# Sign bits of sixteen 64-bit weight tiles masked on POOL, and two instead of three DVE operations in their conversion

## The chip, the core and the metric

The kernel runs on one core of a Trainium2 chip. TensorE (PE) multiplies, VectorE (DVE), ScalarE (ACT) and GpSimd (POOL) work elementwise, SyncE (SP) issues most transfers. Each engine works off its own row of instructions in order and waits for others by semaphores. The metric is the device time of one execution in microseconds (us); lower is better.

## The reference

Three stages follow each other on 6016 rows of 256: the real part of a two-dimensional Fourier transform, then two feed-forward layers of width 2048.

```python
X = np.fft.fft(np.fft.fft(x, axis=1), axis=2).real          # x: 2 x 3008 x 256
h = X @ w_in                                                # layer one, 256 -> 2048
g = np.maximum(h, 0.0) + alpha * np.minimum(h, 0.0)
x = g @ w_out                                               # 2048 -> 256
h = x @ w_in2                                               # layer two
g = h * (1.0 / (1.0 + np.exp(-h)))
out = g @ w_out2
```

The weights w_in, w_out, w_in2 and w_out2 come as 64-bit floats. The kernel gets them as pairs of 32-bit words and makes 32-bit floats of them itself.

## The kernel before

**Stages.** First a part of the Fourier transform is computed (the psU, psB and psP matmuls), then a loop of 96 steps does layer one: 6 blocks of columns (c) by 16 slices of the width (m). Layer two follows from about 500 us on. Steps 0 to 15 are the first block, and in them the weights of layer one arrive, are converted and, for w_in, mixed with the last Fourier matrix.

**One step of layer one** (`step1`): PE makes two products, psh, of three matmuls each. DVE computes h (L588), a sum and a difference in place in PSUM (L589, L591), ACT the negative parts r (L590, L592), and DVE adds them to the products (L594, twice: the first r and the second r). Then `close1`: ACT rounds r to gh (L610), POOL computes the rest, gl = r - gh (L611, the lo part), and second products pso (L626) of gh and gl are put in a queue; PE takes some of them between the psh products of the next steps. Three banks of PSUM serve psh, one bank (tag x) serves psW, psS, psB and others in turn.

**A conversion** (`narrow`): raw words arrive by DMA. ACT scales the high words into y (L227) and the low words in place (L228). Then DVE shifts y left by three (L233), adds the scaled low words (L235, shown as ISA or CUSTOM) and puts the sign bit of the high word in (L237). For w_in, y is the tile wq, and `mix_w` follows: matmuls psW (L536), ACT's hi part (L538), DVE's lo part (L551), and column sums psS (L542). For w_out, `halves` follows: ACT's hi part (L281) and POOL's lo part (L282). Three conversions lie before step 0. The other thirteen of layer one go with steps 0 to 11 and 13, w_in in steps 0, 2, 4, 6, 8 and 10 (even steps), w_out in 1, 3, 5, 7, 9, 11 and 13 (odd steps). The weights of layer two are converted later, from about 220 us on.

**What sets the order.** Everything is issued from one program in which the conversions are generators. They are advanced at fixed places of a step: EARLY at its start, AMID between the two psh products, MID1 between the two L594, MID2 and MID3 behind the second, LATE at the end. The counter `now[0]` is the step; `NF` is 16.

Of the kernel before, what the change touches and what calls it, by code (L numbers as in the profile page):

```python
# [14 lines left out]
ALU = mybir.AluOpType  # L15
# [10 lines left out]
NF = DFF // P  # L26
KG = 2
CK = 8
NC = B * H1 // CK
# [68 lines left out]
def kernel(  # L98
# [16 lines left out]
    V, A, G, T = nc.vector, nc.scalar, nc.gpsimd, nc.tensor  # L115
# [40 lines left out]
    def wtile(shape, dtype, name, tag):  # L156
        return work.tile(shape, dtype, name=name, tag=tag, bufs=BUFS[tag])
# [10 lines left out]
    EARLY, AMID, LATE, BANK, MID1, MID2, MID3 = range(1, 8)  # L168
# [11 lines left out]
    now, taken = [0], set()  # L180
# [17 lines left out]
    def load64(src, raw, eng=nc.sync):  # L198
        eng.dma_start(raw.rearrange("p a n t -> p a (n t)"), src.bitcast(I32))

    def place_raw():
        while started and held[3] == BUFS["raw"]:
            yield EARLY
        held[3] += 1

    def narrow(src, finish, raw=None, lead=0, y=None, ready=lambda: True):

        held[0] += 1
        mine = raw is None
        if mine:  # L210
            yield from place_raw()
            raw = wtile([P, *src.shape[1:], 2], I32, "raw64", "raw")
            load64(src, raw)
            for _ in range(LOAD if lead > 1 else 1 if not started else 2 if now[0] < NF else 1 + lead):
                yield EARLY
        low, high = raw[:, :, :, 0], raw[:, :, :, 1]
        while not ready():
            yield EARLY
        own = y is None
        while own and lead and held[1] == BUFS["y"]:  # L220
            yield EARLY
        held[1] += own
        y = wtile(list(low.shape), F32, "y64", "y") if own else y()
        yi = y.bitcast(I32)
        if started:
            yield AMID
        A.activation(y, high.bitcast(F32), AF.Copy, scale=2.0 ** -112)  # L227
        A.activation(low, low.bitcast(U32), AF.Copy, scale=2.0 ** -29)  # L228
        if now[0] >= NC * NF or not started:
            yield LATE  # L230
        far = NF <= now[0] < NC * NF
        yield MID2 if far else MID1
        V.tensor_scalar(yi, yi, 3, None, op0=ALU.logical_shift_left)  # L233
        yield MID2
        V.tensor_tensor(yi, yi, low, op=ALU.add)  # L235
        yield MID2 if far else MID3
        V.scalar_tensor_tensor(yi, high, -2147483648, yi, op0=ALU.bitwise_and, op1=ALU.bitwise_or)  # L237
        held[0] -= 1
        held[3] -= mine
        if lead >= 0 and started and now[0] < NC * NF:  # L240
            for _ in range(2 if now[0] else 1):
                yield EARLY
            yield AMID
        else:
            for _ in range(1 + lead):
                yield EARLY
        yield from finish(y)
        held[1] -= own
# [4 lines left out]
    def keep_back(src, key):  # L253
        def finish(y):
            stash[key] = dram.tile(list(y.shape), F32, name="stash_{}{}".format(*key))
            nc.sync.dma_start(stash[key], y)
            return
            yield

        return narrow(src, finish)  # L260
# [28 lines left out]
    def narrow_wout(src, dst, tag, n, lead=0, raw=None):  # L289

        q, m = divmod(2 * n, 4)

        def place():
            if m == 0:
                dst[q] = keep.tile([P, 4, 2, D], F32R, name=f"{tag}o{q}", tag=f"{tag}{q}")
            return dst[q][:, m:m + 2, 0, :], dst[q][:, m:m + 2, 1, :]

        if ("o", n) in stash and tag == "wA":
            return bring_back(("o", n), halves(place, (tag, n)), lead)
        return narrow(rows_wout(src, n), halves(place, (tag, n)), raw, lead)  # L300
# [14 lines left out]
    def narrow_win2(p, lead=0):  # L315
        def finish(y):

            a = y.rearrange("p k (m f) -> p k m f", m=2)
            four = y.rearrange("p k (m f) -> p (k m) f", m=2)
            while held[2]:  # L320
                yield EARLY
            held[2] = 1
            w = wi2[p] = place_win2(p)
            s = t1.rearrange("p (i f) -> p i f", i=4)
            A.activation(w[:, :4, 0], four, AF.Copy)
            SE.tensor_tensor(s[:, 0], a[:, 0, 1], a[:, 1, 1], op=ALU.add)
            SE.tensor_tensor(s[:, 1], s[:, 0], a[:, 0, 0], op=ALU.subtract)
            SE.tensor_tensor(s[:, 2], a[:, 0, 0], a[:, 0, 1], op=ALU.subtract)
            SE.tensor_tensor(s[:, 3], a[:, 1, 0], s[:, 1], op=ALU.subtract)
            G.tensor_tensor(w[:, :4, 1], four, f32(w[:, :4, 0]), op=ALU.subtract)  # L330
            for _ in range(1 + lead):
                yield EARLY
            A.activation(w[:, 4:, 0], s, AF.Copy)
            G.tensor_tensor(w[:, 4:, 1], s, f32(w[:, 4:, 0]), op=ALU.subtract)
            held[2] = 0

        if ("i", p) in stash:
            return bring_back(("i", p), finish, lead)
        return narrow(rows_win2(p), finish, None, lead)
# [789 lines left out]
```

## Time and profile before

| | |
|---|---|
| three runs | 977.17, 977.41, 981.92 us (median 977.41) |
| profiled execution | 981.92 us, of it 980.1 us span from the first to the last instruction |
| PE, DVE, ACT, POOL busy | 97%, 73%, 61%, 52% of the span |
| mean granted TensorE clock | 0.993 of full speed |
| L233, L235, L237 in the first 130 us | 16 each, 0.42, 0.69 and 0.69 us by the median |
| POOL L611 (gl) in steps 0 to 15 | 16 of 2.17 us |

In an order of time each row has the start in us from the span's beginning, the duration in us, the engine, line and operation, the tiles written and read, and their shape; in brackets stands how long the engine had been idle before and what released it. Durations include the time in which an operation was held up after its start; with operations that overlap in the pipeline the next one starts before the bar of the last ends.

### The profile page before, as it was taken

Reading aid. Unit: us, or ns where it says so; the run is one execution under the profiler, and the core shown is the slowest. Engines: PE = TensorE matmul, PEld = TensorE weight load, DVE = VectorE, ACT = ScalarE, POOL = GpSimd, SP = SyncE. Lnnn points to the kernel's source line nnn. Section 1 sums busy time; section 2 is a strip of 40 time slices with the busy share of each in tenths; the row PEclk is TensorE's granted clock in tenths of the full one; section 3 lists DMA queues with packets and bytes.
Section 4 is the critical chain, followed back from the end, with each engine's and each line's share of the span. In section 5 each row is a group of like instructions: output and inputs, shape, how many; then the busy total and the mean of one; then the engine's idle time right before and its main releaser. Section 6 shows DMA issues by size and latency. Waiting matters only on the chain.

```text
span 980.1 us, 12471 instructions
## 1 busy us (share of the span) xinstructions
PE 953.3 (97%) x4374; PEld 797.4 (81%) x4374; DVE 711.5 (73%) x1102; ACT 594.7 (61%) x1010; POOL 509.5 (52%) x329
## 2 busy tenths in 40 slices
PE   9899899999999999999999999999999999999998
PEld 8788778878878878778789988888888888888886
DVE  4688877679989989998766766576576566657554
ACT  5566656666666656665676665566565565556654
POOL 0244567765444546898995643354254254335322
PEclk9799999999999999999999999999999999999999
DMA  9401103233344120010010020010000001001001
GB/s 338 156 1 43 43 25 81 76 79 107 94 120 131 55 65 23 22 64 22 22 42 24 1 81 1 1 43 1 1 12 32 1 1 43 1 1 44 1 1 43
DMA packets 30862, 47.59 MB, mean 49 GB/s; under 512 B 3312, under 2 KB 13392, under 8 KB 30544
## 3 DMA queue, kind: packets, MB, share of 16 engines
q1 hardware_dynamic: 30512, 46.41, 14.7%
q8 instruction: 34, 0.56, 0.2%
q10 hardware_dynamic: 288, 0.39, 0.1%
q14 instruction: 28, 0.23, 0.1%
HBM read 33.28 MB, written 13.51 MB: 48 GB/s over the span
## 4 chain that ended last, share of the span: by engine, by line
PE 78%; DVE 10%; ACT 4%; POOL 3%; issue 2%; DMA 1%; SPq 0%; ACTq 0%; DVEq 0%; POOLq 0%
PE pso L814 26%; PE psh L746 23%; PE pso L626 16%; PE psh L580 9%; DVE r L594 4%; ACT r L590 2%; POOL gl L611 2%; DVE psh L589 1%; PE psW L536 1%; DMA stash_o<-y 1%; DVE h L588 1%; PE psB L418 1%; DVE y L237 1%; DVE x L638 1%; ACT gh L610 1%
## 5 line engine op out<-in xcount | busy, mean ns | idle before, releaser
L767 DVE TENSOR_TENSOR ring<-ring,psh 128x512 f32<-128x512 f32 (+1 forms) x336 | 222.2, 674 | 167.8 <-PE psh L746 156.5
L814 PE MATMUL pso<-ghl,wAo 128*128 128x512 f32 (+1 forms) x1152 | 309.8, 385 | 0.0
L611 POOL TENSOR_TENSOR gl<-r,gh 128x1024 fp32r<-128x1024 f32 (+1 forms) x96 | 227.0, 2365 | 149.5 <-ACT gh L610 104.4
L746 PE MATMUL psh<-ts,wi 128*128 128x512 f32 (+1 forms) x1008 | 279.0, 385 | 0.0
L758 POOL TENSOR_TENSOR ghl<-ring,ghl 128x512 fp32r<-128x512 f32 (+1 forms) x96 | 137.3, 1431 | 252.4 <-ACT ghl L753 172.4
L814 PEld LDWEIGHTS pso<-ghl,wAo 128*128 128x128 f32 x1152 | 216.2, 188 | 40.7
L770 ACT ACTIVATE ring<-ring 128x512 f32<-128x512 f32 (+1 forms) x192 | 119.3, 621 | 176.5 <-DVE ring L767 174.6
L746 PEld LDWEIGHTS psh<-ts,wi 128*128 128x128 f32 x1008 | 189.1, 188 | 35.5 <-DVE r L594 0.3
L626 PE MATMUL pso<-gh,wo_o 128*128 128x512 f32 (+1 forms) x768 | 188.2, 386 | 3.2 <-POOL wo_o L282 3.1
L580 PE MATMUL psh<-pq,wa 128*128 128x512 f32 (+1 forms) x576 | 167.5, 400 | 5.8 <-DVE r L594 5.8
L626 PEld LDWEIGHTS pso<-gh,wo_o 128*128 128x128 f32 x768 | 144.0, 188 | 31.5 <-POOL wo_o L282 4.4
L594 DVE SCALAR_TENSOR_TENSOR r<-r,al,psh 128x512 f32<-128x512 f32 (+1 forms) x192 | 134.1, 734 | 16.7 <-ACT r L590 5.6
L610 ACT ACTIVATE gh<-r 128x1024 fp32r<-128x1024 f32 (+1 forms) x96 | 100.3, 1044 | 68.2 <-DVE r L594 67.8
L580 PEld LDWEIGHTS psh<-pq,wa 128*128 128x128 f32 x576 | 106.4, 191 | 30.1 <-DVE r L594 10.7
L753 ACT ACTIVATE ghl<-ring 128x512 fp32r<-128x512 f32 (+1 forms) x192 | 119.0, 620 | 6.2
L626 PE MATMUL pso<-gl,wo_o 128*128 128x512 f32 (+1 forms) x384 | 102.4, 388 | 2.8 <-POOL gl L611 2.8
L590 ACT ACTIVATE r<-psh 128x512 f32<-128x512 f32 (+1 forms) x96 | 56.5, 588 | 79.5 <-DVE psh L589 73.1
L589 DVE TENSOR_TENSOR psh<-h,psh 128x512 f32<-128x512 f32 (+1 forms) x96 | 65.8, 685 | 45.6 <-PE psh L580 41.2
L626 PEld LDWEIGHTS pso<-gl,wo_o 128*128 128x128 f32 x384 | 71.9, 188 | 18.3 <-POOL gl L611 4.6
L758 DVE TENSOR_TENSOR ghl<-ring,ghl 128x512 fp32r<-128x512 f32 (+1 forms) x96 | 77.1, 803 | 4.0 <-ACT ghl L753 3.6
L588 DVE SCALAR_TENSOR_TENSOR h<-pb,wst,psh 128x512 f32<-128x512 f32 (+1 forms) x96 | 70.1, 730 | 1.4 <-ACT pb L992 1.4
L591 DVE TENSOR_TENSOR psh<-h,psh 128x512 f32<-128x512 f32 (+1 forms) x96 | 65.2, 679 | 0.0
(91 smaller groups left out, 667.1 us busy)
## 6 DMA issues: line engine op xcount, KB each, us to landing
raw<-in_w_in SPq DMA_DIRECT2D x16, 512.0 KB, 5.5
raw<-in_w_out SPq DMA_DIRECT2D x16, 512.0 KB, 4.8
out_dram<-ob SPq DMA_DIRECT2D x20, 256.0 KB, 2.2
x<-in_x SPq DMA_DIRECT2D x7, 512.0 KB, 10.1
xr<-in_x SPq DMA_DIRECT2D x16, 192.0 KB, 2.4
tmid<-ev SPq DMA_DIRECT2D x48, 64.0 KB, 1.8
ur<-tmid SPq DMA_DIRECT2D x12, 256.0 KB, 4.1
stash_o<-y SPq DMA_DIRECT2D x8, 256.0 KB, 3.9
```

The source lines that it names most:

```text
L580: T.matmul(t[:, :w], wa[q][:, mm, eo, a, :], pq[c][:, 2 * eo + bb, :w], start=n == 0, stop=n == 2)
L588: V.scalar_tensor_tensor(t[:, :w], pb[c][:, :w], wst[:, m, 0:1], ps[0][:, :w], op0=ALU.mult, op1=ALU.add)
L594: V.scalar_tensor_tensor(r[:, s, :w], r[:, s, :w], al[:, m:m + 1], ps[s][:, :w], op0=ALU.mult, op1=ALU.add)
L610: A.activation(hi[:, :, :w], r[:, :, :w], AF.Copy)
L611: G.tensor_tensor(lo[:, :, :w], r[:, :, :w], f32(hi[:, :, :w]), op=ALU.subtract)
L626: T.matmul(po[c][s][k][:, :w], wo1[q][:, mm, a, k * P:(k + 1) * P], g[:, s, :w], start=m == 0 and a == 0 and g is hi, stop=m == NF - 1 and ...
L746: T.matmul(bank[j][:, :w], wi2[p][:, FORMS[j], a], t[:, :w], start=a == 0 and t is hi, stop=t is lo)
L753: A.activation(outs[p, i][:, 0, :w], g[:, :w], AF.Copy)
L758: eng.tensor_tensor(hl[:, 1, :w], g[:, :w], f32(hl[:, 0, :w]), op=ALU.subtract)
L767: V.tensor_tensor(dst[:, :w], a[:, :w], bank[j][:, :w], op=ALU.add)
L770: A.activation(a[:, :w], a[:, :w], AF.Silu)
L814: T.matmul(po[c, 2][s][k][:, :w], wo2[q][:, mm + m, a, k * P:(k + 1) * P], outs[p, i][:, g, :w], start=p == 0 and i < 2 and a == 0 and g == 0,
```

## The change

For conversions that are issued while the step counter is below 16 (all sixteen of layer one), POOL computes in place, from each high word, a word that is -2147483648 where the word is negative and 0 elsewhere. DVE then shifts y and ORs that word in, in one operation, and adds the low words. The other conversions stay as they were. All lines behind the change have numbers higher by 8.

```diff
         if now[0] >= NC * NF or not started:
             yield LATE
-        far = NF <= now[0] < NC * NF
-        yield MID2 if far else MID1
-        V.tensor_scalar(yi, yi, 3, None, op0=ALU.logical_shift_left)
-        yield MID2
-        V.tensor_tensor(yi, yi, low, op=ALU.add)
-        yield MID2 if far else MID3
-        V.scalar_tensor_tensor(yi, high, -2147483648, yi, op0=ALU.bitwise_and, op1=ALU.bitwise_or)
+        if now[0] < NF:
+            G.tensor_scalar(high, high, 0.0, -2147483648.0, op0=ALU.is_lt, op1=ALU.mult)
+            yield MID1
+            yield MID2
+            V.scalar_tensor_tensor(yi, yi, 3, high, op0=ALU.logical_shift_left, op1=ALU.bitwise_or)
+            yield MID3
+            V.tensor_tensor(yi, yi, low, op=ALU.add)
+        else:
+            far = now[0] < NC * NF
+            yield MID2 if far else MID1
+            V.tensor_scalar(yi, yi, 3, None, op0=ALU.logical_shift_left)
+            yield MID2
+            V.tensor_tensor(yi, yi, low, op=ALU.add)
+            yield MID2 if far else MID3
+            V.scalar_tensor_tensor(yi, high, -2147483648, yi, op0=ALU.bitwise_and, op1=ALU.bitwise_or)
```

The row of DVE in step 3 of the kernel before (the tile y_454 is the converted w_out, raw_144 its words):

```order
L594 SCALAR_TENSOR_TENSOR r<-r,al,psh 128x450
L233 TENSOR_SCALAR y_454<-y_454 128x512
L594 SCALAR_TENSOR_TENSOR r<-r,al,psh 128x450
L235 ISA y_454<-raw_144,y_454 128x1024
L237 SCALAR_TENSOR_TENSOR y_454<-raw_144,y_454 128x512
L551 TENSOR_TENSOR wa_403<-psW,wa_403 128x2x2x128
```

And after the change:

```order
L602 SCALAR_TENSOR_TENSOR r<-r,al,psh 128x450 x2
L235 SCALAR_TENSOR_TENSOR y_454<-y_454,raw_144 128x512
L237 ISA y_454<-raw_144,y_454 128x1024
L559 TENSOR_TENSOR wa_403<-psW,wa_403 128x2x2x128
L596 SCALAR_TENSOR_TENSOR h<-pb,wst,psh 128x450
```

The shift between the two r is gone, and the operation that takes in the sign stands first, ahead of the add.

The row of POOL from just ahead of step 0 to step 5 in the kernel before (the L611 are the lo parts of steps 0, 1, 2, then of 3 and 4; between them L282 is the lo part of the tile y_376, converted in step 1):

```order
L282 TENSOR_TENSOR wo_o_328<-y_242,wo_o_328 128x2x256
L611 TENSOR_TENSOR gl<-r,gh 128x2x450 x3
L282 TENSOR_TENSOR wo_o_328<-y_376,wo_o_328 128x2x256
L611 TENSOR_TENSOR gl<-r,gh 128x2x450 x2
L282 TENSOR_TENSOR wo_o_577<-y_454,wo_o_577 128x2x256
```

And after the change, in steps 2 to 4:

```order
L232 TENSOR_SCALAR raw_140<-raw_140 128x512
L619 TENSOR_TENSOR gl<-r,gh 128x2x450
L290 TENSOR_TENSOR wo_o_328<-y_376,wo_o_328 128x2x256
L232 TENSOR_SCALAR raw_144<-raw_144 128x512
L619 TENSOR_TENSOR gl<-r,gh 128x2x450
L232 TENSOR_SCALAR raw_146<-raw_146 128x512
```

In an odd step the sign stands behind L290 (L282 before) and ahead of the lo part of the same step. In step 13 the rows read alike (raw_861 behind the lo part of y_853):

```order
L290 TENSOR_TENSOR wo_o_979<-y_853,wo_o_979 128x2x256
L232 TENSOR_SCALAR raw_861<-raw_861 128x512
L619 TENSOR_TENSOR gl<-r,gh 128x2x450 x2
L290 TENSOR_TENSOR wo_o_979<-y_955,wo_o_979 128x2x256
L619 TENSOR_TENSOR gl<-r,gh 128x2x450
```

Before, the first of these L619 (L611) followed L290 (L282) directly. The sign waits for ACT's first scaling (L227), DVE's shift waits for the sign.

## Rows read from the trace of the kernel before

**Rows 1.** The page: busy us, share of the span, instructions of each engine.

```profile
PE 953.3 (97%) x4374; PEld 797.4 (81%) x4374; DVE 711.5 (73%) x1102; ACT 594.7 (61%) x1010; POOL 509.5 (52%) x329
```

**Rows 2.** Table of stretches: length, then busy us of PE, PEld, DVE, ACT, POOL.

```profile
47.00:59.00 12.00, 11.90 (x64) 10.67 (x63) 11.00 (x19) 7.66 (x14) 6.76 (x4) 1.00 0.00 1
...
130.00:980.00 850.00, 837.55 (x3774) 695.47 (x3772) 615.15 (x931) 518.94 (x861) 461.70 (x298) 1.00 0.13 39
```

**Rows 3.** Order of time, DVE, step 4: start, duration, line, operation.

```profile
60.47 0.42 DVE L233 TENSOR_SCALAR wq<-wq 128x512 int32<-128x512 int32 x1
60.80 0.68 DVE L594 SCALAR_TENSOR_TENSOR r<-r,al,psh 128x450 f32<-128x450 f32 x1
61.40 0.69 DVE L235 CUSTOM_DVE_ANT_0 wq<-raw,wq 128x1024 uint16<-128x1024 uint16 x1
...
62.73 0.42 DVE L437 TENSOR_TENSOR pq<-psB,pq 128x256 fp32r<-128x256 f32 x1
```

**Rows 4.** Order of time, PE, behind step 4.

```profile
63.20 0.61 PE L542 MATMUL psS<-ones,wq 128*128 128x2 f32 x4 [1.83 <-DVE pq L437]
...
65.43 3.31 PE L536 MATMUL psW<-wq,cwt 128*128 128x256 f32 x8
```

**Rows 5.** Table of stretches, one us; the number behind POOL is the granted clock.

```profile
65.00:66.00 1.00, 1.00 (x4) 0.82 (x4) 0.74 (x2) 1.00 (x4) 1.00 (x1) 0.50 0.00 0
```

**Rows 6.** Order of time, ACT and DVE, the last conversion before step 0.

```profile
26.46 0.60 ACT L538 ACTIVATE wa<-psW 128x512 fp32r<-128x512 f32 x1 [0.22 <-PE psW L536]
27.30 0.69 DVE L551 TENSOR_TENSOR wa<-psW,wa 128x512 fp32r<-128x512 f32 x1
```

**Rows 7.** Order of time, DVE, behind the conversions of steps 1 and 5.

```profile
47.57 0.63 DVE L589 TENSOR_TENSOR psh<-h,psh 128x450 f32<-128x450 f32 x1 [0.44 <-PE psh L580]
...
69.41 0.69 DVE L551 TENSOR_TENSOR wa<-psW,wa 128x512 fp32r<-128x512 f32 x1 [0.35 <-ACT wa L538]
```

**Rows 8.** Order of time, step 3: POOL, DVE, ACT, DVE, POOL.

```profile
53.76 1.30 POOL L282 TENSOR_TENSOR wo_o<-y,wo_o 128x512 fp32r<-128x512 f32 x1
54.42 0.92 DVE L233 TENSOR_SCALAR y<-y 128x512 int32<-128x512 int32 x1
55.97 0.96 ACT L610 ACTIVATE gh<-r 128x900 fp32r<-128x900 f32 x1 [1.14 <-DVE r L594]
56.57 0.69 DVE L237 SCALAR_TENSOR_TENSOR y<-raw,y 128x512 int32<-128x512 int32 x1
57.06 2.19 POOL L611 TENSOR_TENSOR gl<-r,gh 128x900 fp32r<-128x900 f32 x1 [2.00 <-issue]
```

**Rows 9.** Order of time, step 13 and the start of step 14: POOL, DVE.

```profile
113.12 1.27 POOL L282 TENSOR_TENSOR wo_o<-y,wo_o 128x512 fp32r<-128x512 f32 x1
113.65 1.02 DVE L233 TENSOR_SCALAR y<-y 128x512 int32<-128x512 int32 x1
115.90 0.69 DVE L237 SCALAR_TENSOR_TENSOR y<-raw,y 128x512 int32<-128x512 int32 x1
117.51 0.63 DVE L589 TENSOR_TENSOR psh<-h,psh 128x450 f32<-128x450 f32 x1 [0.32 <-PE psh L580]
```

**Rows 10.** Order of time, POOL and DVE, a conversion of layer two.

```profile
394.31 2.40 POOL L611 TENSOR_TENSOR gl<-r,gh 128x1024 fp32r<-128x1024 f32 x1
395.45 1.82 DVE L237 SCALAR_TENSOR_TENSOR y<-raw,y 128x512 int32<-128x512 int32 x1
```

**Rows 11.** Groups by line on POOL, first 130 us: busy us, mean ns.

```profile
L972 POOL TENSOR_TENSOR row<-u_all,cbt 128x512 f32<-128x512 f32 x1 | 1.1, 1059 | 9.0 <-ACT u_all L953 9.0
L890 POOL MEMSET zero<- 128x512 f32 x1 | 0.5, 525 | 0.3 <-POOLq L1104 0.3
```

**Rows 12.** Order of time, step 7: POOL, DVE, POOL.

```profile
77.85 1.29 POOL L282 TENSOR_TENSOR wo_o<-y,wo_o 128x512 fp32r<-128x512 f32 x1
79.23 0.68 DVE L594 SCALAR_TENSOR_TENSOR r<-r,al,psh 128x450 f32<-128x450 f32 x1 [0.40 <-ACT r L590]
81.97 2.20 POOL L611 TENSOR_TENSOR gl<-r,gh 128x900 fp32r<-128x900 f32 x1 [2.83 <-ACT gh L610]
```

## The prediction

> **What bounds the kernel now.** I read the page first, then the table of stretches, then the order of time on DVE, PE, POOL and ACT in the first 130 us. The page says that PE is busy for 97% of the span and DVE for 73% [rows 1]. That is an average. The change acts only on conversions made before step 16, all of them in the first 116 us, and there the table shows another picture: from 47 to 59 us DVE is busy 11.00 of 12 us, while behind 130 us PE has 837.55 of 850 us [rows 2]. So what this change gives or takes in the first stretch moves the start of a stretch that PE fills, and goes into the end time nearly one to one.
>
> Inside the first stretch DVE and PE take turns. In step 4 DVE's row runs without a gap through L233, the second r, L235, L237 (not listed, it fills the 1.33 us between 61.40 and 62.73) and L437 [rows 3]; PE stands still until L437 has freed the one bank that psS needs, 1.83 us [rows 4]. So time taken out of DVE's row ahead of L437 reaches PE whole.
>
> **What is removed.** One TENSOR_SCALAR (L233) per conversion, 16 of them: 3 before step 0, 13 in steps 0 to 11 and 13. Its bar is 0.42 us, but the next operation starts 0.33 us after it: 60.47 to 60.80 [rows 3]. I take 0.33 us for each. The two that remain are an operation with two inputs and the add, the same forms as L235 and L237 in the other order; together they keep their 1.33 us (61.40 to 62.73).
>
> Where does 0.33 us arrive? Not in steps 1 and 5: behind step 1 DVE waits 0.44 us for PE anyway, and in step 5 L551 waits 0.35 us for ACT's half of the mix, which waits for PE [rows 7]. It arrives in steps 0, 2, 4, 6, 7, 8, 9, 10 and 11 (3 and 13 are reckoned apart): 9 x 0.33 = 3.0 us. Of the three before step 0 only the last stands in front of something: L551 at 27.30. It also needs ACT's L538, which ends at 26.46 + 0.60 = 27.06 [rows 6], so 0.2 us is left. **Gain: 3.2 us.**
>
> **What is added on POOL.** One TENSOR_SCALAR of 128x512 int32 per conversion, in POOL's row behind the lo part of the step before and, in odd steps, behind L282. The trace has no such operation. Its bounds: a memset of the same size, which reads nothing, took 0.53 us, and L972, which reads two tensors, 1.06 us [rows 11]; L282 took 1.30 us [rows 8]. I call the duration S and take 1.06, from the nearest operation that reads and computes; 0.53 to 1.3 are my likely ends, since a conversion from and to integers may cost more than a second input. The Trainium skill, GPSIMD Engine Reference, section "Engine selection", advises elementwise work on VectorE, but says that POOL is roughly at line rate with one input; from its 1.2 GHz that is an estimate of 512 / 1.2 = 0.43 us and a start. By it the sum below would come out near zero and not on the slow side; no row here shows a one-input operation on POOL that reads.
>
> **The new wait.** DVE's first operation now waits for POOL; behind it in DVE's row stand the add, L551 or L437, and the next step's h, and for these PE waits. In most steps the sign is ready. Without L233 the shift stands 1.2 us behind the first r. In even steps POOL is free when the lo part ends (step 4: 57.06 + 2.19 = 59.25 [rows 8]), and the shift would stand at 60.47 + 0.60 = 61.07: 1.82 us of cover. In odd steps L282 comes first (step 7: 77.85 + 1.29 = 79.14) and the shift would stand at 79.23 + 1.20 = 80.43 [rows 12]: 1.29 us of cover. With S = 1.06 these steps wait for nothing, and the cost is zero; the cover is POOL's idle time, and above S = 1.3 the odd steps begin to pay.
>
> Two steps have no cover. **Step 3:** L282 ends at 53.76 + 1.30 = 55.06 [rows 8]. The second r would now start at 54.42, the shift at 55.02, but the sign ends at 55.06 + 1.06 = 56.12. Meanwhile ACT's gh can follow the second r: 54.42 + 0.68 + 0.96 = 56.06, and the lo part on POOL may start 0.13 us later, as now, near 56.2. So shift, add and lo part meet. How such a meeting goes is shown at 395 us: POOL's lo part runs from 394.31 to 396.71, and L237, begun at 395.45, takes 1.82 us where it takes 0.69 [rows 8, 10]: it ends 0.56 us behind POOL's operation. If the shift comes first (56.17 to 56.85), the lo part follows at about 56.75 and holds to 58.9, and the add ends at 59.4. Before, L237 ended at 56.57 + 0.69 = 57.26 (L233 itself had there been stretched to 0.92 us by L282). **Loss: 2.1 us.** If the lo part comes first, shift and add both stand behind it, and the next sign can slip between them: 58.4, 58.9, 60.0, 60.5, a loss of 3.2 us. With S = 0.53 the add still meets the lo part: 56.3 + 2.15 + 0.56 = 59.0, a loss of 1.7 us.
>
> **Step 13** is alike: L282 ends at 114.39, the sign at 115.45; the second r at 113.65, gh done at 115.3, the lo part ready at 115.4 [rows 9]. The add then ends near 118.7 instead of 115.90 + 0.69 = 116.59, 2.1 us later, less the 0.32 us that DVE waited for PE behind it. **Loss: 1.8 us** (1.3 with S = 0.53, 2.0 with the lo part first). Nothing else is moved: the order of PE, ACT and SP is the same; the library load of POOL only stands earlier in a row that idles until 10 us.
>
> **Sum:** 3.2 - 2.1 - 1.8 = -0.7 us, slower. The profiled execution took 981.92 us with a span of 980.1, 1.8 us outside; on it this gives 982.6. That execution is the longest of the three, so I carry the difference to the median: 977.41 + 0.7 = 978.1 us. The bounds: S = 0.53 gives 3.2 - 1.7 - 1.3 = +0.2 (977.2 us); the lo part first in both steps gives 3.2 - 3.2 - 2.0 = -2.0 (979.4 us).
>
> **The rivals.** (1) *The meeting costs nothing*: the sign is short and the shift and add slip ahead of the lo part. Then 3.2 us stay: 974.2 us. For it: L237 at 56.57 overlaps the start of the lo part at 57.06 by 0.2 us and keeps its 0.69 us [rows 8]. Against it: the stretched L237 [rows 10]. (2) *The clock*: behind the pause ahead of 63.20 the granted clock is 0.50, 1.2 GHz, from 65 to 66 us, and the mix at 65.43 takes 3.31 us [rows 4, 5]; at 2.4 GHz it would take no less than half, so up to 1.7 us hang on it. Longer pauses behind steps 3 and 13 may bring one or two more such stretches: 979.8 to 981.5 us. Shorter pauses might save this one; with all of rival 1 that is 3.2 + 1.7 = 4.9, 972.5 us, the only way to 0.5%. (3) *The sign is long*. From S = 1.9 on, the add of steps 7, 9 and 11 also meets the lo part (step 7: the add would start after 81.97 [rows 12]), 2.5 us each. With S = 2.17, as the largest POOL operation of the stage, that is 3 x 2.5 for these, some 5 and 3 us for steps 3 and 13, and nearly all gains of the odd and most of the even steps gone: about 14 us, 991 us. For it: the operation converts integers, compares and multiplies, with two constants; against it: it reads half as much as L611 and has one input. The Trainium skill, SBUF — State Buffer, section "Who interferes with whom", has whichever of the two engines starts first holding the shared pair for its whole instruction; by that rule a long sign would also hold a DVE operation with two SBUF inputs, which no row shows for a one-input operation on POOL. (4) *The change doesn't do what it says*: the order speaks against it, DVE loses 16 rows and POOL gains 16.
>
> **How the numbers follow.** A difference of 0.5% (4.9 us) is about what a measurement of this kernel can tell from no change; the three runs alone span 4.7 us. Forecast (977 to 979.4): 0.50. Rival 1: 0.20. Rival 2, slower side: 0.10; its fast side: 0.06. Rival 3: 0.14. Within 0.5% lie forecast, rival 1 and the slow side of rival 2: 0.80; faster 0.06; slower 0.14. The range goes from rival 1 to a little past rival 2: 974.0 to 982.5 us.
>
> **What would show it.** The POOL rows of L232 give S: 0.5 to 1.3 us if I am right. DVE's row of step 4 should read r, r, shift, add, 0.33 us shorter. In steps 3 and 13 shift or add should have a bar of about 1.2 to 2.8 us in place of 0.69, beside a lo part on POOL; nowhere else. If L235 is nowhere longer than 0.7 us, rival 1 holds; if it waits for POOL in all odd steps, rival 3. PE's stretch behind 130 us should be as long as before; if it isn't, I have missed something.

## The result and the profile after

The changed kernel takes 992.31 us (median of four, 989.73 to 995.9), the kernel before, run beside it, 978.35 us (four, 977.17 to 981.92). The ratio is 1.0134, with an interval of 1.0097 to 1.0171: slower by 1.3%, some 13 us, where 0.7 us had been forecast and 982.5 us was the upper end. The third rival, "the sign is long", had put 991 us.

The profiled execution is the longest of the four: 995.9 us with a span of 994.1. Lines are higher by 8. First the page's line of busy times, with columns as in [rows 1]:

```profile
PE 958.1 (96%) x4374; PEld 800.5 (81%) x4374; DVE 718.7 (72%) x1086; ACT 594.5 (60%) x1010; POOL 542.2 (55%) x345
```

The table of stretches, as in [rows 2]:

```profile
47.00:59.00 12.00, 11.93 (x59) 10.35 (x57) 9.42 (x15) 8.39 (x15) 10.95 (x6) 1.00 0.00 1
...
146.00:994.00 848.00, 836.05 (x3767) 694.11 (x3765) 615.60 (x930) 517.93 (x860) 460.91 (x298) 1.00 0.13 39
```

DVE has 16 operations fewer and is nevertheless busy 7.2 us longer, and POOL 32.7 us longer for 16 added operations: 2.0 us each. From 47 to 59 us POOL, not DVE, is now the fuller of the two: 10.95 of 12 us, where it had 6.76. Behind 146 us all is as it was: PE 836.05 of 848 us against 837.55 of 850 us [rows 2]. The loss lies wholly in the stage where the conversions are.

The starts of h in DVE's row, step by step, say where. In us, length of steps from one h to the next, by step number:

| | start of step 0 | even steps 0 to 10, sum | odd steps 1 to 13, sum | step 12 | steps 14, 15 | start of step 16 |
|---|---|---|---|---|---|---|
| before | 35.75 | 32.44 | 44.54 | 3.78 | 7.22 | 123.73 |
| after | 36.87 | 29.35 | 60.53 | 4.50 | 6.81 | 138.06 |

The even steps gain 3.1 us (0.3 to 0.5 each, and 1.2 in step 6: there DVE's operation behind h had waited 0.97 us for PE, which was late from the half clock in step 5 [rows 5], and now waits 0.10 us), the odd ones lose 16.0 us: 3.4 in step 3, 3.1 in step 13, 1.9 to 2.6 in steps 5, 7, 9 and 11, 0.4 in step 1.

All sixteen signs as one line of the trace, with minimum, median and maximum of the duration in ns, first and last start, and under it who waited for them (us, times):

```profile
L232 POOL TENSOR_SCALAR raw<-raw x16: 1988/2008/2432, 11.6 to 126.0; 128x512 int32<-128x512 int32 x16
...
who waited for it (us, times):
  POOL gl L619: 16.4, 8
  DVE y L235: 7.0, 8
  DVE wq L235: 1.1, 1
```

The sign takes 2.0 us, where 1.06 had been taken and 1.3 was the likely upper end [rows 11]. What that does in an odd step shows in step 7, in order of time on POOL, on ACT, then on DVE; it is to be laid beside [rows 12]:

```profile
82.28 1.28 POOL L290 TENSOR_TENSOR wo_o<-y,wo_o 128x512 fp32r<-128x512 f32 x1
83.54 2.00 POOL L232 TENSOR_SCALAR raw<-raw 128x512 int32<-128x512 int32 x1
86.22 2.13 POOL L619 TENSOR_TENSOR gl<-r,gh 128x900 fp32r<-128x900 f32 x1 [0.69 <-POOL raw L232]
...
85.14 0.95 ACT L618 ACTIVATE gh<-r 128x900 fp32r<-128x900 f32 x1
...
83.65 1.28 DVE L602 SCALAR_TENSOR_TENSOR r<-r,al,psh 128x450 f32<-128x450 f32 x2 [0.38 <-ACT r L598]
85.57 0.69 DVE L235 SCALAR_TENSOR_TENSOR y<-y,raw 128x512 int32<-128x512 int32 x1 [0.65 <-POOL raw L232]
86.30 2.61 DVE L237 CUSTOM_DVE_ANT_0 y<-raw,y 128x1024 uint16<-128x1024 uint16 x1
88.83 0.68 DVE L559 TENSOR_TENSOR wa<-psW,wa 128x512 fp32r<-128x512 f32 x1
```

POOL begins the sign as soon as L290 leaves it and ends at 85.54. DVE has its two r done 0.65 us earlier and waits; then the shift runs in its usual 0.69 us. Meanwhile ACT finishes gh, at 86.09, and POOL's lo part, which reads it, starts at 86.22. The add, begun 0.08 us later, has a bar of 2.61 us in place of 0.69: it ends 0.55 us behind the lo part (88.91 against 88.36), not after its own work. So the step pays 0.65 us of waiting and 1.92 us of being held, less 0.33 us for the operation that is gone: 2.24 us, and the table of starts says 2.3.

In step 3 it is the shift that is held (POOL, then DVE; compare [rows 8]):

```profile
55.75 1.99 POOL L232 TENSOR_SCALAR raw<-raw 128x512 int32<-128x512 int32 x1
57.70 2.10 POOL L619 TENSOR_TENSOR gl<-r,gh 128x900 fp32r<-128x900 f32 x1
59.77 2.42 POOL L232 TENSOR_SCALAR raw<-raw 128x512 int32<-128x512 int32 x1
...
57.77 2.57 DVE L235 SCALAR_TENSOR_TENSOR y<-y,raw 128x512 int32<-128x512 int32 x1 [1.94 <-POOL raw L232]
60.38 1.00 DVE L237 CUSTOM_DVE_ANT_0 y<-raw,y 128x1024 uint16<-128x1024 uint16 x1
```

The lo part had been waiting for POOL and starts 0.07 us ahead of the shift. Step 13 is alike: the shift waits 1.28 us and takes 2.61 us.

Over the seven odd steps the waits come to 6.7 us (the line of the waits below), and the held operations to 11.7 us: four adds of 2.54 to 2.61 us and two shifts of 2.57 and 2.61 us in place of 0.69, and 0.3 us of step 3's add. Against 18.4 us stand seven times 0.33 us for the operation removed, the stretched L233 of steps 3 and 13 (together 1.1 us over its 0.42) and the 0.35 us by which DVE had waited in step 5 [rows 7]. That leaves 14.6 of the 16.0 us. Of the other 1.4 us, 0.9 lie in step 13, where DVE waits 1.80 us for PE's psh behind h and had waited 0.93 us before; step 12 is 0.7 us longer besides. Both stand behind a stretch of half clock: ahead of 117.05 PE pauses 2.66 us, and the granted clock then is 0.57 on average from 117 to 121 us, so that three matmuls of psh take 1.47 us. In the kernel before it is 1.00 in these four us, and three such matmuls there, at 116.69, take 0.79 us.

From the table of waits between 34 and 150 us (us in total, times, longest):

```profile
DVE y L235 <- POOL raw L232: 6.7, 7, 1.9
```

PE in order of time behind step 11:

```profile
117.05 0.60 PE L486 MATMUL psR<-cbt,u 128*128 128x64 f32 x2 [2.66 <-DVE wa L559]
117.41 1.47 PE L588 MATMUL psh<-pq,wa 128*128 128x450 f32 x3
```

The stretch behind that pause, the granted clock again behind POOL:

```profile
117.00:121.00 4.00, 3.95 (x13) 3.57 (x14) 2.53 (x5) 1.57 (x4) 0.00 (x0) 0.57 0.24 87
```

The even steps read as predicted, step 4 on DVE:

```profile
63.98 1.28 DVE L602 SCALAR_TENSOR_TENSOR r<-r,al,psh 128x450 f32<-128x450 f32 x2
65.18 0.68 DVE L235 SCALAR_TENSOR_TENSOR wq<-wq,raw 128x512 int32<-128x512 int32 x1
65.90 0.69 DVE L237 CUSTOM_DVE_ANT_0 wq<-raw,wq 128x1024 uint16<-128x1024 uint16 x1
66.50 0.42 DVE L445 TENSOR_TENSOR pq<-psB,pq 128x256 fp32r<-128x256 f32 x1
```

From the first r to the last of the four rows it is 2.52 us, 2.86 before (59.87 to 62.73): 0.34 us less, without a wait.

### The profile page after: what moved, and what is told of

Its sections match the earlier page's. It is cut to its first block, busy times and chain, and to the rows that moved or that the text cites. A ratio compares the mean times of both kernels' runs of the same rounds, so it can differ in the third digit from the quotient of the medians.

```text
span 994.1 us, 12486 instructions
## 1 busy us (share of the span) xinstructions
PE 958.1 (96%) x4374; PEld 800.5 (81%) x4374; DVE 718.7 (72%) x1086; ACT 594.5 (60%) x1010; POOL 542.2 (55%) x345
## 4 chain that ended last, share of the span: by engine, by line
PE 77%; DVE 11%; ACT 4%; POOL 3%; DMA 3%; issue 2%; SPq 0%; ACTq 0%; DVEq 0%; POOLq 0%
PE pso L822 26%; PE psh L754 23%; PE pso L634 16%; PE psh L588 8%; DVE r L602 3%; ACT r L598 2%; DVE psh L597 2%; POOL gl L619 1%; DVE h L596 1%; DVE y L237 1%; DMA raw<-in_w_out 1%; PE psB L426 1%; POOL raw L232 1%; DVE y L235 1%; PE psW L544 1%
## 5 line engine op out<-in xcount | busy, mean ns | idle before, releaser
L619 POOL TENSOR_TENSOR gl<-r,gh 128x1024 fp32r<-128x1024 f32 (+1 forms) x96 | 226.8, 2363 | 128.8 <-ACT gh L618 79.0
L588 PE MATMUL psh<-pq,wa 128*128 128x512 f32 (+1 forms) x576 | 170.3, 405 | 7.5 <-DVE r L602 7.5
```

The lines of the kernel that those rows point to most:

```text
L588: T.matmul(t[:, :w], wa[q][:, mm, eo, a, :], pq[c][:, 2 * eo + bb, :w], start=n == 0, stop=n == 2)
L619: G.tensor_tensor(lo[:, :, :w], r[:, :, :w], f32(hi[:, :, :w]), op=ALU.subtract)
```

## The experiments

The theory after the result: the sign's 2.0 us exceed the odd steps' cover of 1.29 us, and what costs is not so much the wait as that shift and add are pushed onto the lo part, which reads SBUF on POOL while they read two inputs from it. Rivals: POOL as a whole is overloaded, so every added microsecond costs, in the even steps too; the loss grows evenly with the sign's length; the wait alone is the cost; the form with two operations is to blame, not the sign; the clock does it. Ratios are against the kernel before, run on the same chip. Diffs are against the kernel after, but for the first. A line added ahead shifts the line numbers by one.

**What the sign costs by itself.** Eight operations on an unused tile in POOL's row at the start of the kernel before:

```diff
+        G.memset(tall, 0.0)
+        G.tensor_scalar(tpair, tpair, 0.0, -2147483648.0, op0=ALU.is_lt, op1=ALU.mult)
+        G.tensor_scalar(tline, tline, 0.0, -2147483648.0, op0=ALU.is_lt, op1=ALU.mult)
+        G.tensor_scalar(tline, tline, 0.0, None, op0=ALU.is_lt)
+        G.tensor_scalar(tall[:, :512], tall[:, :512], 0.5, None, op0=ALU.mult)
+        G.tensor_scalar(tline[:, :256], tline[:, :256], 0.0, -2147483648.0, op0=ALU.is_lt, op1=ALU.mult)
+        G.tensor_scalar(f32(tpair), f32(tpair), 0.0, 0.0, op0=ALU.min, op1=ALU.mult)
+        G.tensor_scalar(tall[:, 512:], tall[:, 512:], 0.0, 0.0, op0=ALU.min, op1=ALU.mult)
+        G.tensor_tensor(tall[:, :512], tall[:, :512], tall[:, 512:], op=ALU.subtract)
```

(tpair is every second word of the tile, tline its first 512 words, both as int32.)

> The kernel before with eight operations more on POOL in its first 10 us, on a tile that nobody uses yet, while DVE has no work: the sign operation on int32 at every second word, on int32 without gaps, its comparison alone, a float multiplication by one constant, the sign operation on 256 columns, a float operation with two constants (min with 0, then times 0) at every second word and without gaps, and a subtraction of two tiles. If the 2.0 us of the changed kernel are the operation's own, the first row takes 2.0 us here too, with DVE idle; if another engine held it up there, it is near 1 us. If the cost is integer conversion, the float forms take 1.1 us or less and the integer ones 2.0; if it is the second constant, both forms with one constant take about 1.1 us and all with two 2.0; if it is a fixed start, 256 columns take over 1.5 us. The whole time stays within 1 us of before.

One execution took 980.42 us. POOL's row in order of time; DVE has nothing to do until 10.20 us, so the first four rows and most of the fifth ran beside an idle DVE:

```profile
2.22 1.99 POOL L897 TENSOR_SCALAR trial<-trial 128x512 int32<-128x512 int32 x1
4.29 1.92 POOL L898 TENSOR_SCALAR trial<-trial 128x512 int32<-128x512 int32 x1
6.29 1.50 POOL L899 TENSOR_SCALAR trial<-trial 128x512 int32<-128x512 int32 x1
7.87 1.49 POOL L900 TENSOR_SCALAR trial<-trial 128x512 f32<-128x512 f32 x1
9.45 1.08 POOL L901 TENSOR_SCALAR trial<-trial 128x256 int32<-128x256 int32 x1
10.61 2.00 POOL L902 TENSOR_SCALAR trial<-trial 128x512 f32<-128x512 f32 x1
12.69 2.00 POOL L903 TENSOR_SCALAR trial<-trial 128x512 f32<-128x512 f32 x1
14.78 1.29 POOL L904 TENSOR_TENSOR trial<-trial 128x512 f32<-128x512 f32 x1
```

So the 2.0 us are the operation's own and no contention. Integers do not make it long (1.50 us, and 1.49 with floats, with one constant each), nor does the stride (1.92 us without), nor a fixed start (1.08 us for half the columns). The second constant with its operation adds 0.4 us with integers (1.92 against 1.50); the two float rows with two constants, 2.00 us each, ran beside DVE's first operations. Even with one constant it takes 1.49 us, longer than a subtraction of two tensors, 1.29 us.

**The same without the sign.** POOL's operation left out:

```diff
-            G.tensor_scalar(high, high, 0.0, -2147483648.0, op0=ALU.is_lt, op1=ALU.mult)
```

> The changed kernel without POOL's sign operation, so the sign bit is not prepared (a part of the computation is left out): DVE has its two operations and waits for nothing. My sum for the gain alone is 3.2 us, so about 975 where before has 978. If the loss of the changed kernel lies in DVE's new pair of operations or their order, this stays slower than before, at 985 or more.

Measured: 974.34 us, ratio 0.9944 [0.9923, 0.9966]. Taking one operation off DVE is worth 5.4 us, more than the 3.2 us summed. By the starts of h, steps 3 and 13 give 1.8 us (there L233 had been stretched too, and the sum had set these steps apart), and steps 5 and 6 give 2.0 us where 0.33 had been counted: the stretch of half clock at 65 to 69 us [rows 5] is gone; another, at 118 to 122 us, costs 1.6 us in step 16.

**A sign of half the length.** Half of the columns only:

```diff
-            G.tensor_scalar(high, high, 0.0, -2147483648.0, op0=ALU.is_lt, op1=ALU.mult)
+            half = high[:, :, :low.shape[2] // 2]
+            G.tensor_scalar(half, half, 0.0, -2147483648.0, op0=ALU.is_lt, op1=ALU.mult)
```

> The changed kernel with the sign operation on half of the columns (the other half of the signs is left out), so that S is near 1.06 us, the value of my forecast. If only the duration was mis-sized, the time is that of the forecast, 977 to 980 us: odd steps 5 to 11 don't wait for POOL, steps 3 and 13 still meet the lo part. If the cost comes from any POOL operation in that place, whatever its length, it stays above 985 us.

Measured: 981.05 us, ratio 1.0008 [0.9994, 1.0023]. The sign has 1.10 us by the minimum and 1.11 by the median, near the 1.06 of the forecast, and this is the kernel that was predicted: 0.7 us slower by the sum, 0.8 by the ratio, whose interval runs from 0.6 us faster to 2.3 us slower. DVE's rows of steps 3, 7 and 13 in order of time:

```profile
54.62 0.69 DVE L236 SCALAR_TENSOR_TENSOR y<-y,raw 128x512 int32<-128x512 int32 x1 [1.05 <-POOL raw L233]
55.35 2.50 DVE L238 CUSTOM_DVE_ANT_0 y<-raw,y 128x1024 uint16<-128x1024 uint16 x1
...
78.69 0.69 DVE L236 SCALAR_TENSOR_TENSOR y<-y,raw 128x512 int32<-128x512 int32 x1
79.42 0.69 DVE L238 CUSTOM_DVE_ANT_0 y<-raw,y 128x1024 uint16<-128x1024 uint16 x1
...
112.27 2.64 DVE L236 SCALAR_TENSOR_TENSOR y<-y,raw 128x512 int32<-128x512 int32 x1 [1.17 <-POOL raw L233]
```

Steps 3 and 13 meet the lo part, the add in one and the shift in the other; steps 5 to 11 wait for nothing. That is what the prediction had worked out for a sign of this length; that the sum agrees as well is in part luck (see the account of the prediction).

**Only the even steps.** The new path for w_in alone:

```diff
-        if now[0] < NF:
+        if now[0] < NF and lead < 0:
...
-            far = now[0] < NC * NF
+            far = NF <= now[0] < NC * NF
```

> The new pair and the sign operation only in conversions of w_in (even steps), the three operations of before in those of w_out (odd steps). With S = 2.0 the even steps have 1.8 us of cover, so the gain is 6 x 0.1 to 0.33 us: 976 to 977.5 where before has 978, same by measurement. If 2 us more on POOL cost by themselves, by late lo parts for PE, it is slower by some 4 to 6 us, since the even steps have six of the thirteen.

Measured: 977.61 us, ratio 0.9987 [0.9972, 1.0002]. Signs of 1.99 us (the median of eight) in the six even steps and ahead of step 0 make DVE wait 0.8 us in all (0.09 to 0.27 us in steps 2, 4, 6, 8 and 10), and the time does not rise. POOL's load as such is not the bound; it is the odd steps.

**The same wait, without the meeting.** The lo part of the odd steps replaced by two memsets, which read nothing:

```diff
-        G.tensor_tensor(lo[:, :, :w], r[:, :, :w], f32(hi[:, :, :w]), op=ALU.subtract)
+        if c == 0 and m % 2 and m < 14:
+            for _ in range(2):
+                G.memset(f32(lo[:, :, :w]), 0.0)
+        else:
+            G.tensor_tensor(lo[:, :, :w], r[:, :, :w], f32(hi[:, :, :w]), op=ALU.subtract)
```

> The changed kernel, but the lo part of steps 1, 3, 5, 7, 9, 11 and 13 is written by two memsets on POOL in place of the subtraction (the low-order part of these seven slices is left out). POOL is taken for about 1.7 us as before, but it reads nothing. If the loss is the meeting at the port (the add or the shift held up until the lo part has been read), no DVE bar of L235 or L237 is longer than 0.9 us beside these memsets, and only the waits for the sign are left: 0.7 us in steps 5 to 11, 1.9 and 1.3 us in steps 3 and 13, less the gain of the even steps: 978 to 983 us. If waiting for POOL's 2.0 us makes up the loss by itself, the time stays at 988 us or more.

Measured: 981.01 us, ratio 1.0018 [1.0005, 1.0031], 11.3 us under the kernel after. Step 7 on POOL, then on DVE:

```profile
78.55 2.03 POOL L232 TENSOR_SCALAR raw<-raw 128x512 int32<-128x512 int32 x1
80.49 1.79 POOL L621 MEMSET gl<- 128x900 f32 x2
...
80.61 0.69 DVE L235 SCALAR_TENSOR_TENSOR y<-y,raw 128x512 int32<-128x512 int32 x1 [0.64 <-POOL raw L232]
81.33 0.69 DVE L237 CUSTOM_DVE_ANT_0 y<-raw,y 128x1024 uint16<-128x1024 uint16 x1
```

All adds of the tiles y as one line, with minimum, median and maximum:

```profile
L237 DVE CUSTOM_DVE_ANT_0 y<-raw,y x8: 691/693/694, 25.6 to 117.3; 128x1024 uint16<-128x1024 uint16 x8
```

The wait for the sign is the same 0.64 us (7.1 us over the odd steps, 6.7 in the kernel after), and POOL is at work beside shift and add as before, but they take their 0.69 us. So of the loss about 11 us are the meeting and what follows from it (the granted clock is 1.00 from 117 to 121 us here), near the 11.7 us of held bars, and the waits are what the gain of the change pays for. The memsets are 0.3 us shorter than the lo part and don't wait for gh, so the two kernels differ by a little more than the read. The Trainium skill, SBUF — State Buffer, section "Who interferes with whom", says that a DVE instruction with two SBUF inputs contends with a GpSimd instruction that reads SBUF, and not with one that only writes it; the trace agrees for these two: 2.61 us beside the subtraction, 0.69 us beside the memsets. It does not for the sign, which reads SBUF too: the next experiment shows the add beside it.

**The old three operations behind a sign on POOL.** Now the last operation waits instead of the first:

```diff
             yield MID1
+            V.tensor_scalar(yi, yi, 3, None, op0=ALU.logical_shift_left)
             yield MID2
-            V.scalar_tensor_tensor(yi, yi, 3, high, op0=ALU.logical_shift_left, op1=ALU.bitwise_or)
-            yield MID3
             V.tensor_tensor(yi, yi, low, op=ALU.add)
+            yield MID3
+            V.scalar_tensor_tensor(yi, high, -2147483648, yi, op0=ALU.bitwise_and, op1=ALU.bitwise_or)
```

> The changed kernel with POOL's sign operation, but with DVE's three operations of before (shift between the two r, add, then the sign, which still comes out right from the prepared word). Only the last one waits for POOL, 1.05 us later in the row than the changed kernel's first one. DVE has more work than in the changed kernel and POOL the same. If the place of the wait and the meeting decide, it is faster than the changed kernel: steps 5 to 11 no longer wait, steps 3 and 13 meet the lo part at 2.4 us each, so 980 to 984 us. If 2.0 us more on POOL cost by themselves (late lo parts for PE), it stays at 988 us or more.

Measured: 988.34 us, ratio 1.0084 [1.0056, 1.0113], longer than expected. In steps 1 and 5 to 11 the last operation waits for nothing and takes 0.69 us. Steps 3 and 13 meet the lo part, as with the half sign. On DVE, and PE's pause behind step 13:

```profile
57.97 2.59 DVE L238 SCALAR_TENSOR_TENSOR y<-raw,y 128x512 int32<-128x512 int32 x1 [0.69 <-POOL raw L232]
...
120.30 2.61 DVE L238 SCALAR_TENSOR_TENSOR y<-raw,y 128x512 int32<-128x512 int32 x1 [0.68 <-POOL raw L232]
...
130.71 2.23 PE L635 MATMUL pso<-gh,wo_o 128*128 128x450 f32 x7 [2.46 <-POOL wo_o L291]
```

Each costs 2.6 us. The rest lies at half clock. By the starts of h, step 2 is 1.0 us and step 16 is 2.0 us longer than before; behind the pause of 2.46 us that ends at 130.71 PE's granted clock is 0.50 from 132 to 135 us, and ahead of step 2 it is low from 39 to 47 us (in the kernel before from 41 to 45). The expectation had counted the meetings and not the pauses that follow them.

This run also shows that not every operation of POOL holds DVE. Its add, L236 with two inputs from SBUF, begins while POOL is at the sign in steps 1, 3, 7, 9, 11 and 13. Step 7 on POOL and DVE:

```profile
82.40 2.04 POOL L232 TENSOR_SCALAR raw<-raw 128x512 int32<-128x512 int32 x1
...
84.08 0.69 DVE L236 CUSTOM_DVE_ANT_0 y<-raw,y 128x1024 uint16<-128x1024 uint16 x1
```

In these six steps the add takes 0.68 to 0.69 us; in steps 3 and 13 it is done 0.6 us before the sign. So a long sign does not hold DVE by itself, as the third rival had allowed for. In every trace here a conversion's operation with two inputs that begins inside a TENSOR_TENSOR of POOL ends 0.55 us behind it; beside a TENSOR_SCALAR, as the sign is, it takes 0.68 to 1.00 us, and beside the memsets 0.69 to 0.70 us. Why the sign's reads do not hold DVE is not shown.

**The same result from another operation.** On POOL the high words, read as floats, times a column of zeros give a zero with the sign of the word:

```diff
-            G.tensor_scalar(high, high, 0.0, -2147483648.0, op0=ALU.is_lt, op1=ALU.mult)
+            highf = high.bitcast(F32)
+            G.tensor_tensor(highf, highf, u0[:, 64:66].rearrange("p (a o) -> p a o", o=1).to_broadcast(list(high.shape)), op=ALU.mult)
```

> The changed kernel with another operation on POOL that gives the same sign bit: the high words, taken as floats, times a column of zeros (two inputs, one of them a column). By the subtraction and L972 it takes 1.06 to 1.3 us in place of 2.0. If the duration decides, the time is near that of the half operation: steps 5 to 11 wait less than 0.3 us and meet nothing, steps 3 and 13 meet the lo part, 978 to 982 us. If the kind of operation doesn't matter and any sign on POOL costs 10 us, it stays at 988 us or more.

Measured: 980.5 us, ratio 1.0013 [0.9997, 1.0029]. All sixteen signs as a line of the trace:

```profile
L233 POOL TENSOR_TENSOR raw<-raw,u x16: 1031/1048/1489, 13.1 to 113.9; 128x512 f32<-128x512 f32 x16
```

With two inputs it takes 1.05 us, half of the operation with one input and two constants. As with the half sign, steps 3 and 13 meet (the add takes 2.50 and 2.51 us there), the others don't, and the time is that of the half sign.

**And with steps 3 and 13 left as they were.** In addition:

```diff
-        if now[0] < NF:
+        if now[0] < NF and now[0] not in (3, 13):
...
-            far = now[0] < NC * NF
+            far = NF <= now[0] < NC * NF
```

> As the version with times zero, but steps 3 and 13 have the three operations of before and no sign on POOL. If the two meetings were all that stood against the gain, what is left is 9 x 0.33 us and the 0.2 us at the start, perhaps with a shorter pause of PE and so less time at 1.2 GHz: 973 to 976 us where before has 978 to 980, faster by 0.3 to 0.6%. If other losses remain in the odd steps, it is no faster than the version with the sign in even steps alone.

Measured: 974.08 us, ratio 0.9957 [0.9936, 0.9978]: under both kernels, by 0.4% and 1.8%, and equal to the kernel without any sign. No add of the new form is longer than 0.69 us:

```profile
L238 DVE CUSTOM_DVE_ANT_0 y<-raw,y x6: 691/692/693, 25.3 to 100.7; 128x1024 uint16<-128x1024 uint16 x6
```

**A sign of 1.5 us.** One multiplication by the constant 0, to see whether the loss rises evenly or from a threshold:

```diff
-            G.tensor_scalar(high, high, 0.0, -2147483648.0, op0=ALU.is_lt, op1=ALU.mult)
+            highf = high.bitcast(F32)
+            G.tensor_scalar(highf, highf, 0.0, None, op0=ALU.mult)
```

> The changed kernel with the sign made by one multiplication of the high words, taken as floats, by the constant 0: one constant in place of two, so 1.49 us on POOL by the row of the sizes. If the loss has a threshold, the point from which the add of steps 7, 9 and 11 meets the lo part (S = 1.9 by my prediction), these steps only wait some 0.2 to 0.5 us here and meet nothing, and the time is 980.5 to 983 us, like with 1.05 us. If the loss grows evenly with the duration, it lies on the line from 980.5 us at 1.05 to 992.3 us at 2.0, at 986 us.

Measured: 980.36 us, ratio 1.0015 [1.0, 1.0029]. The signs as one line:

```profile
L233 POOL TENSOR_SCALAR raw<-raw x16: 1553/1566/1985, 11.5 to 110.1; 128x512 f32<-128x512 f32 x16
```

DVE in steps 3 and 9, in order of time:

```profile
51.93 2.59 DVE L236 SCALAR_TENSOR_TENSOR y<-y,raw 128x512 int32<-128x512 int32 x1 [1.51 <-POOL raw L233]
...
88.38 0.69 DVE L236 SCALAR_TENSOR_TENSOR y<-y,raw 128x512 int32<-128x512 int32 x1 [0.45 <-POOL raw L233]
89.11 0.69 DVE L238 CUSTOM_DVE_ANT_0 y<-raw,y 128x1024 uint16<-128x1024 uint16 x1
```

Steps 5 to 11 wait 0.15 to 0.45 us, as 1.57 against a cover of 1.29 would have it, and slip ahead of the lo part. The four lengths side by side:

| sign | 1.05 us | 1.11 us | 1.57 us | 2.01 us |
|---|---|---|---|---|
| time | 980.5 | 981.05 | 980.36 | 992.31 |
| ratio to the kernel before | 1.0013 | 1.0008 | 1.0015 | 1.0134 |

A straight line from 1.11 to 2.01 us would give 986.8 us at 1.57; the longest of twelve executions took 984.25. The loss beyond steps 3 and 13 sets in between 1.57 and 2.01 us, where the wait grows long enough for the lo part to be ready.

## Why the prediction was wrong

**The step that failed is "I call the duration S and take 1.06".** It measured 2.0 us. "From the nearest operation that reads and computes" was a guess by kinship, and the kin were two-input operations; on POOL one input and two constants cost more than two inputs. The likely ends, 0.53 to 1.3 us, missed it too. So the range stopped at 982.5 us, with 14 chances in 100 for what lay beyond the threshold, though the duration that decided it stood in no row; the price on that side, 991 us, is what came, but for 1.3 us. That it came so near is in part luck: that rival took most of the even steps' gains as gone, and they stayed (3.1 us); it had 8 us for steps 3 and 13, which lost 6.5; step 5, the half clock behind step 11 and a later start of step 0, which it had not counted, made up for that.

**What hung on S was worked out right.** The covers were 1.82 us in even and 1.29 us in odd steps: with S = 2.0 the odd steps with such a cover wait 0.65 to 0.90 us (0.71 by subtraction). In step 4 the row is 0.34 us shorter (0.33 predicted). Steps 3 and 13 have bars of 2.5 to 2.6 us. The start at which further steps join, "from S = 1.9 on", agrees with nothing at 1.57 and all of it at 2.01. Step 5 joins as well, which the rival had left out, and step 1 pays its wait of 0.67 us but does not meet the lo part, whose gh is late there. With S brought to the value that had been assumed, the ratio, 1.0008, is that of the forecast, but not term by term. By the starts of h in the profiled execution of the half sign, the steps up to 16 other than 3 and 13 gain 6.1 us, where 3.0 had been summed; steps 3 and 13 lose 4.4 us, where it was 3.9; and from step 16 on it takes 0.8 us longer, with the granted clock at 0.50 from 125 to 127 us, for which the sum had nothing. These two executions differ by 0.8 us the other way (spans of 979.3 and, before, 980.1), since the kernel before was profiled in a long one; so the balance is no closer than the spread of the executions.

**The gain of 3.2 us was too small**: 5.4 us without the sign. Setting steps 3 and 13 apart had hidden that L233's own stretch there, 0.92 and 1.02 us in place of 0.42 [rows 8, 9], goes with it, and the half clock of step 5 was priced only in a rival.

**The rivals.** That the meeting costs nothing is excluded: with the memsets in place of the lo part the time was 11.3 us less. The clock as a rival of its own is not needed for most of the result, since the held bars and waits carry 14.6 of the odd steps' 16.0 us, but it moved in the way described; no run holds it fixed, so its share, some 1.6 us in steps 12 and 13, is argued and not shown. In the kernel after, the stretch of half clock lies at 63 to 66 us, ahead of the mix, which at full clock takes 1.89 us (68.96) where it took 3.31 [rows 4]: 1.4 us of the 1.7 that were put on it:

```profile
68.96 1.89 PE L544 MATMUL psW<-wq,cwt 128*128 128x256 f32 x8
```

Two new ones, at 117 and 134 us, follow steps 11 and 13. Of the start, 0.2 us sooner was predicted; DVE's L559 there does start 0.5 us sooner (26.78 against 27.30 [rows 6]), but PE's half clock begins at 28 us instead of 30, and step 0 starts 1.1 us later. How much of this start belongs to the change stays open: it differs from execution to execution (below).

## What to carry to other kernels

Moving work to an idle engine costs nothing as long as its result comes within the cover, which one can read from the rows; the duration of the moved operation belongs into an idle slot of that engine's row and under a measurement before it goes into a sum. A wait that is a little too long may cost little by itself and much by what becomes ready meanwhile: look for the next operation on the other engine that would then run beside it, and for a row of such a pair: here POOL's two-input subtraction held DVE's two-input operations, and its one-input sign and its memsets did not. Where a gain of some tenths of a us recurs in many steps and a loss sits in two of them, leave these two out.

## What the runs showed that was not expected

- On POOL 128x512 with one input takes 1.49 to 1.57 us with one constant (1.57 at every second word) and 1.92 to 2.00 us with two, as int32 and as float; a subtraction of two tensors takes 1.29 us and a product with a broadcast column 1.05 us. The Trainium skill, GPSIMD Engine Reference, section "Engine selection", calls one input roughly line rate; by the page's 1.2 GHz an estimate is 0.43 us, and the measurement decides against it.
- An operation of DVE that was held also lengthens POOL's next: the sign behind the lo part of steps 3, 5, 7 and 9 takes 2.42 to 2.43 us in place of 2.00, and in step 3 DVE's L237 has 1.00 in place of 0.69 (59.77 and 60.38 in the rows of step 3).
- The start of step 0 lies at 32.0 to 32.6 us in two of the profiled executions (the sign of 1.5 us, the even steps only), where the granted clock is 1.00 at 30 to 31 us, and at 34.6 to 36.9 us in the others, where it is 0.50 to 0.90. A part of the spread of one kernel's executions, 976.9 to 982.6 us for the kernel before, may come from there; that was not tried.
